# A retention layer and a gated feed-forward on one core: one load, two gate blocks and a few sums change places in a hand-written order

## The chip, the cores and the metric

One core of a Trainium2 chip. The metric is device time in microseconds of one execution. The program is built from a language in which each instruction goes to the queue of one engine (TensorE, VectorE, ScalarE, GpSimd, SyncE) in the order in which the program issues it; semaphores between the engines are set from the data that they share.

## The reference

Two layers, one after the other, on q, k, v of (4 batches, 8 heads, 768 steps, 64):

```python
gamma = 1.0 - 2.0 ** (-5.0 - np.arange(H))
for t in range(S):
    state = gamma * state + np.einsum('bhd,bhe->bhde', k[:, :, t], v[:, :, t])
    y[:, :, t] = scale * np.einsum('bhd,bhde->bhe', q[:, :, t], state)
x = y.transpose(0, 2, 1, 3).reshape(B * S, H * D)          # 3072 x 512
gate = 1.0 / (1.0 + np.exp(-(x @ w_gate)))                 # w_gate 512 x 1536
val = x @ w_val                                            # w_val  512 x 1536
out = (gate * val) @ w_out                                 # w_out 1536 x 512
```

## The kernel before, in words

**Chunks, pairs, tiles.** The 768 steps are cut into six chunks of 128, one for each tile `t` (0 to 5). A tile has the four batches of a chunk, so 512 tokens, in two *pairs* `P = 2t` and `2t + 1` of two batches each; `c` (0, 1) is the batch within a pair. So pairs 2 and 3 are tile 1, pairs 4 and 5 are tile 2.

**The first layer for a pair.** `load` (L96, GpSimd's queue) brings k, q, v of a pair from DRAM. k and q are turned: pairs 0 to 3 by TensorE (`tp`, L200) with a copy out of the accumulator by ScalarE (`te`, L210), later pairs by a transposing DMA from SyncE's queue (`xk`, `xq`). `sc` (L238) computes the scores of one batch into two accumulator banks, `mk` (L243, VectorE) multiplies a bank by the decay mask, `in` (L253) multiplies q by the state so far, `ia` (L258) adds masked scores times v, `yo` (L273, VectorE) writes the result as the tile's `xT`. `kt` scales k by the decay, `sm` (L280) computes the new part of the state into the one bank `z`, `zs` (L290, VectorE) adds it to the state and `zo` (L295, ScalarE) writes it out for the matmuls.

**The second layer for a tile.** Early tiles: `gm`/`vm` (whole blocks of gate and value, 512 tokens) with `sg` and `mu`, or half blocks of 256 tokens: `ag`, `av` (left half of the columns), `bg`, `bv` (right half), each with sigmoid (`as`, `bs`) and product (`am`, `bm`). From tile 2 on, the products of gate, value and output are done in seven block products in place of eight (Strassen and Winograd's scheme): `gp`, `vp`, `dp`, with the sums of blocks that it needs: of weights (`aw`, `ad`, `dw`, `dd`, `wp`; `ad` and `dd` on VectorE, the others on GpSimd, L361 and L456), of x (`xs` on VectorE, `xg` on GpSimd, L371), of the hidden layer (`hs` on VectorE, `hg` on GpSimd, L474). `gc`, `vc`, `dc` (ScalarE) copy a product out of its bank, `ga`, `va`, `da` (VectorE) add the next to it.

**The order** is written out by hand: `ORDER` has one string for each tile, and each token is a step and its number. `tp7` is number 7 = 2P + i: q (i = 1) of pair 3; `mk10` is 4P + 2c + i: pair 2, batch 1, first bank; `sc`, `in`, `ia`, `yo` count 2P + c; `sm`, `zs` count pairs; `ag2` starts with hidden block 2. A `-` or `+` behind a token moves its tile number by one. A step in capitals does its matmuls whole (128 rows by 128 columns of the array), in small letters as two halves of 64 columns (L305 and L309 in `mm`):

```python
for i in range(2):
    half = slice(i * D, (i + 1) * D)
    nc.tensor.matmul(o[half], left[:, half], right, skip_group_check=True, **kw)
```

**Memory.** Every accumulator bank but `z` comes from `bank()`: the string `PLACES["ff"]` says which of seven banks the next request gets, and its first writer waits until the bank's last tenant has been read. `PLACES["st"]` does the same for the masked scores. The loads of k, q and v of pairs 2 to 5 and of the output weights are issued ahead of `ORDER` on GpSimd's queue; the sums that GpSimd does follow in the same queue.

Of the kernel before, what the change touches and what calls it, by code (L numbers as in the profile page):

```python
# [17 lines left out]
def kernel(  # L18
# [38 lines left out]
        "gs": "01234501234503215034203502345102354130524301453201540321453034035412031524",  # L57
        "maskd": "01",
        "ff": (
            "012345601230465102346523105246310542631405314056321602341562034163412045632516523560132601562306"  # L60
            "251062562015020324512065630653102651604250142343624015405400652016203541034046326504510416035253"
            "245132541351025162405034123406520512341234160532120605410531324"
        ),
        "qkT": "010231230123",
        "kt": "0101100101",
        "st": "012345670123456702134675120346752104637563245710",
        "xT": "010101",
        "hT": "010101",
        "scr": "010101101001101010010101010101",
# [12 lines left out]
    def held_in(P, n):  # L82
        held = {"k": kn, "q": qn, "v": vn}[n]
        t, j = divmod(P, 2)
        if (n, t) not in lands:
            lands[n, t] = place(ld, [C, 4 * H, D], BF16, tag=n, name=n + "n")
        for i in range(2):
            held[2 * t + i] = lands[n, t][:, i * 2 * H:(i + 1) * 2 * H, :]
        return held[P]

    def load(P, *what, pairs=1):
        t, j = divmod(P, 2)
        for n in what:
            held_in(P, n)
            x = {"k": k, "q": q, "v": v}[n]
            nc.gpsimd.dma_start(out=lands[n, t][:, j * 2 * H:(j + pairs) * 2 * H, :],  # L96
                                in_=x[2 * j:2 * (j + pairs), :, t * C:(t + 1) * C, :].rearrange("b h s d -> s (b h) d"))
# [85 lines left out]
    qkT, kt, sc, st, y, zz, za, xT = {}, {}, {}, {}, {}, {}, {}, {}  # L183
# [377 lines left out]
    def hold(P):  # L561
        nc.gpsimd.tensor_copy(kept[:, :2], qkT[P][:, :, 1, NP - 1, C - 1])

    def hold_for_sums(t):
        nc.gpsimd.tensor_copy(kept[:, 2:3], hs[t][:, 2, NFF // 2 - 1, :1])
# [53 lines left out]
    for s in range(4):  # L619
        load_out(s)  # L620
    load(4, "k", "q", "v")
    load(5, "k", "q", "v")

    STEPS = {
        "gm": lambda t, n: up(t, n, 0),
# [38 lines left out]
        "lk": lambda t, P: load(P, "k", pairs=2),  # L664
        "lq": lambda t, P: load(P, "q", pairs=2),
        "lv": lambda t, P: load(P, "v", pairs=2),
        "ho": lambda t, P: hold(P),
        "hi": lambda t, n: hold_for_sums(t),
        "xk": lambda t, P: xbar(P, 0),
# [128 lines left out]
```

## Time and profile before

| | |
|---|---|
| median of 3 runs | 215.74 us (215.36 to 215.93) |
| profiled execution | 215.9 us, of which the span from first to last instruction is 214.2 |
| granted TensorE clock | 1.00 |
| instructions | 7187 |
| busy: TensorE, VectorE, ScalarE, GpSimd | 204.6, 189.2, 147.5, 139.5 us |
| moved by DMA | 25.38 MB, mean 118 GB/s |

Rows below have the start from the span's beginning, the duration, the engine (PE = TensorE, PEld = its weight loads, DVE = VectorE, ACT = ScalarE, POOL = GpSimd, SP = SyncE), the line of the kernel, the operation and its tiles as out<-in, the shapes, and the count of instructions merged into the row. What stands in brackets is the idle time of the engine just before, and what ended it. The chain of waits follows the run back from its last instruction, at each step to what released it.

### The profile page before, as it was taken

What the parts mean: (1) busy time and instruction counts of PE and PEld (TensorE: products, weight loads), DVE (VectorE), ACT (ScalarE), POOL (GpSimd) and SP (SyncE); (2) the same over time, 40 slices, a digit from 0 to 9 for tenths busy, and PEclk for the clock granted to TensorE, in tenths of its full rate; (3) what the DMA queues carried; (4) which work ended last, traced back from release to release, by engine and by line L of the source; (5) the groups of instructions that cost most, each with busy time, mean ns of one, the idle gap of its engine ahead of it and who ended that gap; (6) DMA issues with size and microseconds to landing.
All of it is one profiled execution on the core that took longest, in us unless ns stands there. A gap on an engine that the chain in (4) does not pass through costs nothing.

```text
span 214.2 us, 7187 instructions
## 1 busy us (share of the span) xinstructions
PE 204.6 (96%) x2938; PEld 177.3 (83%) x2938; DVE 189.2 (88%) x406; ACT 147.5 (69%) x396; POOL 139.5 (65%) x145
## 2 busy tenths in 40 slices
PE   6778999999999999999999999999999999999994
PEld 6555555778888998899988889998899988888883
DVE  6587979989999999979999899999999999968971
ACT  6384466543994389786869798787768969577731
POOL 8977784679999946699764279875618537024500
PEclk9999999999999999999999999999999999999999
DMA  9999999999995999969995129998121000023305
GB/s 125 143 170 194 195 173 165 183 199 159 159 132 33 98 156 143 204 126 157 170 227 115 49 99 163 159 105 127 49 101 52 3 0 3 0 50 70 75 25 183
DMA packets 103922, 25.38 MB, mean 118 GB/s; under 512 B 93904, under 2 KB 101072, under 8 KB 103888
## 3 DMA queue, kind: packets, MB, share of 16 engines
q0 software_dynamic: 81104, 13.90, 84.6%
q1 hardware_dynamic: 22640, 10.88, 28.6%
q8 instruction: 23, 0.38, 0.7%
q10 hardware_dynamic: 144, 0.13, 0.2%
q14 instruction: 11, 0.09, 0.1%
HBM read 28.31 MB, written 6.29 MB: 162 GB/s over the span
## 4 chain that ended last, share of the span: by engine, by line
PE 76%; DMA 14%; POOL 4%; DVE 3%; issue 1%; ACT 0%; ACTq 0%; DVEq 0%; POOLq 0%
PE ff L305 41%; PE ff L309 29%; DMA qn<-in_q_dram 6%; DMA wg<-in_moe_w_gate_dram 4%; DMA vn<-in_v_dram 4%; PE ff L238 2%; PE ff L258 2%; DVE scr L414 1%; POOL kn L96 1%; PE z L280 1%; DVE gs L435 1%; DVE xT L273 1%; POOL vn L96 1%; POOL qn L96 1%; POOL kn L104 1%
## 5 line engine op out<-in xcount | busy, mean ns | idle before, releaser
L420 POOL TENSOR_TENSOR hT<-gs,scr 128x512 bf16<-128x512 f32 x17 | 22.1, 1302 | 21.4 <-ACT gs L440 9.0
L430 ACT COPY gs<-ff 128x256 f32<-128x256 f32 x72 | 25.6, 377 | 11.1 <-PE ff L305 5.7
L409 ACT COPY scr<-ff 128x256 f32<-128x256 f32 x72 | 25.2, 375 | 6.5 <-PE ff L309 3.6
L414 DVE TENSOR_TENSOR scr<-scr,ff 128x512 f32<-128x512 f32 (+1 forms) x48 | 25.6, 547 | 3.5 <-ACT scr L409 1.3
L435 DVE TENSOR_TENSOR gs<-gs,ff 128x512 f32<-128x512 f32 (+1 forms) x48 | 25.8, 548 | 3.2 <-PE ff L305 2.0
L510 ACT COPY ob<-ff 128x256 f32<-128x256 f32 x48 | 17.7, 375 | 15.2 <-PE ff L305 8.9
L243 DVE TENSOR_TENSOR st<-ff,maskd 128x512 bf16<-128x512 f32 x40 | 25.7, 682 | 0.9 <-PE ff L238 0.9
L440 ACT ACTIVATE gs<-gs 128x512 f32<-128x512 f32 (+1 forms) x48 | 24.7, 530 | 2.3 <-DVE gs L435 2.2
L309 PE MATMUL ff<-xT,wg 128*64 128x256 bf16 (+1 forms) x268 | 24.2, 308 | 0.0
L309 PEld LDWEIGHTS <-wg 128*64 128x64 bf16 x356 | 19.4, 110 | 4.1 <-issue 0.4
L423 POOL TENSOR_TENSOR hT<-gs,scr 128x256 bf16<-128x256 f32 x16 | 11.9, 747 | 15.9 <-ACT gs L440 12.0
L309 PE MATMUL ff<-xT,wv 128*64 128x256 bf16 (+1 forms) x220 | 21.5, 311 | 0.0
L305 PEld LDWEIGHTS <-hT 128*128 128x128 bf16 x198 | 19.2, 98 | 2.7 <-issue 0.2
L305 PE MATMUL ff<-wo,hT 128*128 128x256 bf16 x156 | 21.0, 273 | 0.0
L309 PEld LDWEIGHTS <-wv 128*64 128x64 bf16 x312 | 17.2, 110 | 4.2 <-issue 0.3
L305 PEld LDWEIGHTS <-wv 128*128 128x128 bf16 x184 | 17.7, 98 | 2.4
L305 PEld LDWEIGHTS <-wg 128*128 128x128 bf16 x162 | 15.7, 98 | 3.8 <-issue 1.1
L309 PE MATMUL ff<-xs,ws 128*64 128x256 bf16 x208 | 18.7, 273 | 0.0
L305 PE MATMUL ff<-xT,wv 128*128 128x256 bf16 (+1 forms) x134 | 18.5, 276 | 0.0
L231 ACT ACTIVATE kt<-kn,tabk 128x128 bf16<-128x128 bf16 x48 | 18.3, 405 | 0.1
L309 PEld LDWEIGHTS <-ws 128*64 128x64 bf16 x308 | 17.2, 110 | 0.3
L305 PE MATMUL ff<-xT,wg 128*128 128x256 bf16 x110 | 15.4, 272 | 1.6 <-ACT xT L271 1.6
(118 smaller groups left out, 526.8 us busy)
## 6 DMA issues: line engine op xcount, KB each, us to landing
out_dram<-ob SPq DMA_DIRECT2D x18, 256.0 KB, 3.3
vn<-in_v_dram POOLq DMA_DIRECT2D x6, 256.0 KB, 12.4
wo<-in_moe_w_out_dram POOLq DMA_DIRECT2D x4, 384.0 KB, 14.2
kn<-in_k_dram POOLq DMA_DIRECT2D x3, 512.0 KB, 7.8
qn<-in_q_dram POOLq DMA_DIRECT2D x3, 512.0 KB, 10.0
vn<-in_v_dram POOLq DMA_DIRECT2D x3, 512.0 KB, 11.6
out_dram<-ob SPq DMA_DIRECT2D x11, 128.0 KB, 2.2
kn<-in_k_dram POOLq DMA_DIRECT2D x5, 256.0 KB, 13.4
```

The costliest lines, as they stand in the source:

```text
L231: nc.scalar.activation(to[:, :, h, :], x[:, :, h, :], AX.Copy, scale=tabk[:, 0, h:h + 1])
L243: nc.vector.tensor_tensor(st[P, c, i], sc[P, c][i], (mask0 if P < 2 else maskd)[:, i], op=ALU.mult)
L305: nc.tensor.matmul(o, left, right, skip_group_check=True, **kw)
L309: nc.tensor.matmul(o[half], left[:, half], right, skip_group_check=True, **kw)
L409: nc.scalar.copy(vals[t, g][:, {1: 0, 5: 2, 3: 1}[n]], m[False][:, 256:] if n == 1 else m[True][:, :256])
L414: nc.vector.tensor_tensor(o, o, x, op=ALU.add)
L420: eng.tensor_tensor(h[:, 2 * g], s, vals[t, g][:, 0:2].rearrange("p two n -> p (two n)"), op=ALU.mult)
L423: eng.tensor_tensor(h[:, 2 * g + 1, 256:], s[:, 256:], vals[t, g][:, 2], op=ALU.mult)
L430: nc.scalar.copy(o, pairs[t, g, 0][x][:, :256] if x else pairs[t, g, 0][x][:, 256:])
L435: nc.vector.tensor_tensor(o, o, pairs[t, g, 0][False][:, cols], op=ALU.add)
L440: nc.scalar.activation(o, x, AX.Sigmoid)
L510: nc.scalar.copy(o, fast[t, i][x][:, :256] if x else fast[t, i][x][:, 256:])
```

## The change

Five edits of the order, and one string of places made to match.

1. The load of v for pair 5 is no longer issued with the other loads; a new step `lw` issues it behind `hg6` of tile 0 (a hidden sum on GpSimd).
2. At the end of pair 2: the four masks stand together and in the order 10, 11, 8, 9; `in4` in halves takes the place of `IN4`, ahead of both `ia` steps; the products `mu10` and the block `vm11` stand behind `yo4`.
3. The gate block `ag2` stands ahead of the transposes of pair 3's q (`tp7`), `ag4` ahead of pair 3's scores (`sc6`, `sc7`), and the value block `AV6` ahead of `ia6`, `ia7`.
4. `dc11` and `dc15` of tile 0 stand ahead of `kt46` and `kt44` on ScalarE, `hs7` ahead of `dd17` and `bm4` on VectorE; `xs2` of tile 2 and the weight sum `dd3` stand ahead of sums of tile 1's hidden layer (`hs9`, `hs11`).
5. In tile 2, `sm6` stands behind `gp57` and `gs57` and not ahead of `vp47`.

`PLACES["ff"]` and `PLACES["st"]` are new from the first such step on. Apart from names of banks, the tenants ahead of a request differ only around edits 2 and 3 and around `AV4` to `AV10` of tile 1.

```diff
-    load(5, "k", "q", "v")
+    load(5, "k", "q")
...
+        "lw": lambda t, P: load(P, "v"),
...
-mu6- mu8- mk10- mk8- mk11- wp8 vm10- mu10- wp2 in5 ia5 vm11- IN4 mk9- ia4 yo5 tp6 yo4 aw13 sg11- te6 mu11-
-tp7 te7 dd5 dd15 ag2 ag6 kt24 xk5- as2 sc6 mk12 dd20 sc7 mk15 sm3 ag4 as4 wp5 dd7 ag0 IN7 zs3 VM7- as0 mk13
-mk14 IN6 zo7 sm2- zs2 ia6 yo6 ia7 yo7 AV6 zo4 AV2 AG10
+mu6- mu8- mk10- mk11- mk8- mk9- wp8 vm10- wp2 in5 in4 ia5 ia4 yo5 yo4 vm11- mu10- tp6 aw13 sg11- te6 mu11-
+ag2 tp7 te7 dd5 dd15 ag6 kt24 xk5- as2 ag4 sc6 mk12 dd20 sc7 mk15 sm3 as4 wp5 dd7 ag0 IN7 zs3 VM7- as0 mk13
+mk14 IN6 zo7 sm2- zs2 AV6 ia6 yo6 ia7 yo7 zo4 AV2 AG10
...
-zo6 hg6- BV0
+zo6 hg6- lw5 BV0
...
-bs6 kt46 kt44 dc11- AV4 kt37 am0 BV6 bm0 bm2 wp10 xq5- hs11- dd17 bm4 dc15- hs7- DP13-
+bs6 dc11- dc15- kt46 kt44 AV4 kt37 am0 BV6 bm0 bm2 wp10 xq5- hs11- hs7- dd17 bm4 DP13-
...
-hs8 zo11 gp25+ vc01+ hs9 | hs11- gp21 gp22 xs2 gp01 gp02 ... dp17-- gc05 dd3- gc01
+hs8 dd3 zo11 gp25+ vc01+ xs2+ hs9 | hs11- gp21 gp22 gp01 gp02 ... dp17-- gc05 gc01
...
-vf46 vf56 sm6 vp47 va47 in14 gp57 ga57 gs57 vp57
+vf46 vf56 vp47 va47 in14 gp57 ga57 gs57 sm6 vp57
```

More of the change, by code (lines that the diff above doesn't have):

```diff
@@ L59 @@
         "ff": (
-            "012345601230465102346523105246310542631405314056321602341562034163412045632516523560132601562306"
-            "251062562015020324512065630653102651604250142343624015405400652016203541034046326504510416035253"
-            "245132541351025162405034123406520512341234160532120605410531324"
+            "012345601230465102346523105246310542631405314056321632045631205431542056312643621634012430462136"
+            "240362462304323125402364613641032640635243052151625304534533642306231450315356126435403506314241"
+            "254012450140324062534315021536423402150215063412023634503410125"
         ),
@@ L65 @@
         "kt": "0101100101",
-        "st": "012345670123456702134675120346752104637563245710",
+        "st": "012345670123456701234675210346751204637563145720",
         "xT": "010101",
```

54 rows, old and new, of the table ORDER are left out of this document.

## The prediction

> **What bounds the kernel now.** I read the engines of the page first, then the chain of waits, then the timelines of TensorE, VectorE, ScalarE and GpSimd around the changed steps, and last the DMA issues.
>
> ```profile
> PE 204.6 (96%) x2938; PEld 177.3 (83%) x2938; DVE 189.2 (88%) x406; ACT 147.5 (69%) x396; POOL 139.5 (65%) x145
> ```
>
> TensorE is busy almost throughout; a gain has to show as a wait that it no longer has, or as matmuls that it issues more cheaply. The chain of waits says where the last wait for data is:
>
> ```profile
> 27.54 13.44 DMA qn<-in_q_dram
> ```
>
> That is pair 3's q: it lands at 27.54 + 13.44 = 40.98 us. From there on the chain is nearly all TensorE, with short pieces of VectorE. The stretch that is changed, in TensorE's timeline (start, us, line, xcount):
>
> ```profile
> 37.08 1.03 PE L309 MATMUL ff<-xT,wv 128*64 128x512 bf16 x8
> 37.94 0.39 PE L309 MATMUL ff<-qkT,zbd 128*64 128x128 bf16 x8
> 38.16 0.52 PE L258 MATMUL ff<-st,vn 128*64 128x128 bf16 x8
> 38.49 1.05 PE L309 MATMUL ff<-xT,wv 128*64 128x512 bf16 x8
> 39.48 0.40 PE L305 MATMUL ff<-qkT,zbd 128*128 128x128 bf16 x4
> 39.81 0.41 PE L258 MATMUL ff<-st,vn 128*64 128x128 bf16 x8
> 40.05 0.61 PE L200 MATMUL ff<-ident,kn 128*64 128x128 bf16 x16
> 41.02 0.64 PE L200 MATMUL ff<-ident,qn 128*64 128x128 bf16 x16 [0.36 <-DMA qn<-in_q_dram]
> 41.49 1.91 PE L309 MATMUL ff<-xT,wg 128*64 128x256 bf16 x32
> 43.34 0.62 PE L238 MATMUL ff<-qkT 64*128 64x128 bf16 x16
> 43.89 0.44 PE L280 MATMUL z<-vn,kt 128*64 128x64 bf16 x16
> 44.16 1.92 PE L309 MATMUL ff<-xT,wg 128*64 128x256 bf16 x32
> 46.01 0.40 PE L305 MATMUL ff<-qkT,zbd 128*128 128x128 bf16 x4
> ...
> 47.43 0.44 PE L280 MATMUL z<-vn,kt 128*64 128x64 bf16 x16
> 47.70 0.62 PE L258 MATMUL ff<-st,vn 128*64 128x128 bf16 x16
> 48.25 1.92 PE L305 MATMUL ff<-xT,wv 128*128 128x256 bf16 x16
> ```
>
> In step names these are vm10, in5, ia5, vm11, IN4, ia4, tp6, tp7, ag2+ag6, sc6+sc7, sm3, ag4+ag0, IN7, (VM7, IN6), sm2, ia6+ia7, AV6+AV2. Ends are modelled and overlap the next start, so I count from start to start. A wait for data shows at tp7 only, and all that is gained before 40.98 is worth nothing unless tp7 stops being the next thing that TensorE must do.
>
> **Pair 2's end, up to the first transposes (tp6).** IN4 becomes in4: four full matmuls become eight halves, like in5. in5 takes 38.16 - 37.94 = 0.22 us. IN4 takes 39.81 - 39.48 = 0.33, and vm11 ahead of it takes 39.48 - 38.49 = 0.99 where vm10, of the same form, takes 0.86: 0.13 goes into the change of form. So in4 saves 0.33 + 0.13 - 0.22 = 0.24. ia5 takes 0.33 where ia4 takes 0.24, because its second matmul waits for mask mk11; with mk11 second among the masks that 0.09 goes too. Against it stands a new wait: ia4 now follows ia5 at once and needs the fourth mask, mk9.
>
> ```profile
> 36.36 1.89 DVE L243 TENSOR_TENSOR st<-ff,maskd 128x512 bf16<-128x512 f32 x3
> ```
>
> Three masks in 1.89 us, one of 0.68: a step of 0.605. Four in a row from 36.36 end at 36.36 + 3 x 0.605 + 0.68 = 38.86. TensorE would begin ia4 at 37.94 + 0.22 + 0.22 + 0.24 = 38.62 and finish it at 38.86 + about 0.25 = 39.1. vm11 (0.86) ends at 39.97, so tp6 starts at 39.97, not 40.05: only 0.08 is gained here. What is queued on VectorE behind these masks is yo5, yo4 and, moved behind them, mu10 and mu11; yo4 ends near 39.3 + 0.7 = 40.0 (a step as long as a mask's). Nothing asks for mu10 or mu11 before sc6 takes their banks at 43.6.
>
> **Gate blocks ahead of pair 3's q and scores.** tp6 takes what tp7 takes, 41.49 - 41.02 = 0.47, and ends at 40.44. ag2 (needs yo5 and yo4, done at 40.0) now fills the time until q has landed: a half block is about 0.87 (two take 1.85, of which 0.10 goes to the change of form into the scores). It ends at 41.31, after 40.98, so tp7 doesn't wait: 41.31 to 41.78. ag6 ends at 42.65, ag4, also moved up, at 43.52, and sc6 starts at 43.62. The copies out of the transposes run under those blocks:
>
> ```profile
> 40.71 2.01 ACT L210 COPY qkT<-ff 128x1024 bf16<-128x1024 bf16 x2 [2.34 <-PE ff L200]
> ```
>
> One takes 1.0; the second can start at about 41.95 and ends at 43.0, ahead of 43.62. If this cover were gone (tp7 0.6 later), the scores would wait. sc6, sc7 and sm3 take 44.16 - 43.34 = 0.82, so ag0 starts at 44.44, against 44.16 + 0.87 = 45.03 before: a lead of 0.59. IN7 follows after 46.01 - 45.03 = 0.98 at 45.42, and sm2 after another 1.42 at 46.84.
>
> **AV6 ahead of ia6 and ia7.** sm2 has one accumulator bank, which zs3 must have read.
>
> ```profile
> 43.77 0.69 DVE L243 TENSOR_TENSOR st<-ff,maskd 128x512 bf16<-128x512 f32 x1 [0.68 <-PE ff L238]
> ```
> ```profile
> 45.38 1.12 DVE L290 SCALAR_TENSOR_TENSOR za<-za,tabz,z 128x128 f32<-128x128 f32 x4
> 46.41 1.28 DVE L243 TENSOR_TENSOR st<-ff,maskd 128x512 bf16<-128x512 f32 x2
> 47.91 1.12 DVE L290 SCALAR_TENSOR_TENSOR za<-za,tabz,z 128x128 f32<-128x128 f32 x4 [0.22 <-PE z L280]
> ```
>
> VectorE waited for the scores at 43.77; they come 43.62 - 43.34 = 0.28 later, so zs3 ends at 46.50 + 0.28 = 46.78, just in time for sm2, and the masks for ia7 end at 47.69 + 0.28 = 47.97. In the old order ia7 would stand at about 47.3 and wait 0.6; AV6 fills that. Its price is two more changes of form: ia6+ia7 to AV6 costs about 0.10 (48.25 - 47.70 = 0.55 for two times 0.22), and a return about as much, so 0.22 together. sm2 46.84 to 47.11, AV6 from 47.23 to 48.10, ia6 and ia7 from 48.20 to 48.64, AV2 at 48.76, against 48.25 + 0.87 = 49.12. **The lead that is left is 0.36 us.** The Trainium skill ("TensorEngine Tiling (Array Packing)", Key Properties) says that changing the tiling mode drains the engine; by it alone, IN4 to in4 saves two changes, AV6 adds two, and that pair would come to nothing. The rows agree that a change costs; the gain of this part comes from tp7's wait.
>
> VectorE has no lead here (zs2 begins at 47.9 in both) and needs none: yo7 is done near 50.3, and the first block on the right half of the columns follows AV2, AG10 and a product, at about 51.2.
>
> **Pair 5's v load.** On GpSimd's queue:
>
> ```profile
> 46.41 1.14 POOL L96 DMA_DIRECT2D vn<-in_v_dram  x1 [0.59 <-DMA wo<-in_moe_w_out_dram]
> ```
> ```profile
> 60.77 1.34 POOL L474 TENSOR_TENSOR hT<-hT 128x512 bf16<-128x512 bf16 x1
> ```
>
> Without it the queue goes on at 46.41 - 0.59 = 45.82, not at 47.55: every sum up to hg6 comes 1.73 earlier, hg6 ends at 62.11 - 1.73 = 60.38, and the load is issued there; what is behind it is up to 0.6 earlier. No gain of TensorE's follows, since it doesn't wait for these sums. The load's first reader is sm5:
>
> ```profile
> 69.58 0.44 PE L280 MATMUL z<-vn,kt 128*64 128x64 bf16 x16
> ```
>
> With the lead this is 69.22, so the load may take 8.8 us from issue to landing.
>
> ```profile
> vn<-in_v_dram POOLq DMA_DIRECT2D x6, 256.0 KB, 12.4
> ...
> kn<-in_k_dram POOLq DMA_DIRECT2D x3, 512.0 KB, 7.8
> ```
> ```profile
> vn<-in_v_dram POOLq DMA_DIRECT2D x1, 256.0 KB, 17.5
> ```
>
> The last row is this load itself, in its old place, at the end of a full queue. The bounds are 7.8 (twice the bytes, median of three later loads) and 17.5. At 60.38 only q of pair 5 is ahead of it, so I take 7.8 or less: landing by 68.2, cost nothing, about 1 us to spare.
>
> **The rest.** dc11, dc15 ahead of two kt, hs7 ahead of dd17, and xs2 and dd3 ahead of hidden sums reorder the same work on ScalarE and VectorE; they let TensorE's readers come 0.36 earlier without finding them late.
>
> ```profile
> 78.19 0.42 DVE L371 TENSOR_TENSOR xs<-xT,xs 128x512 bf16<-128x512 bf16 x1
> 78.52 0.29 DVE L361 TENSOR_TENSOR ws<-wg,ws 128x256 bf16<-128x256 bf16 x1
> ```
>
> I cost them at nothing; bounds are +-0.7, the two rows' sum, should a reader of one or of what they displace stand waiting. sm6 moved behind gp57:
>
> ```profile
> 109.02 0.61 DVE scr L414
> 109.62 0.04 issue
> 109.67 0.41 PE ff L309 x4
> ```
> ```profile
> 109.11 0.41 PE L309 MATMUL ff<-xs,wg 128*64 128x256 bf16 x4
> ```
>
> gp57 to vp57 takes 0.56 where the four matmuls need 0.22: 0.34 of waiting for VectorE (va56). sm6 can fill 0.25 of it, but gp57 in turn has to wait for the addition that ends at 109.02, so it can't move up, and vp57 starts when va56 ends, as before. Taken as nothing, bounds 0 and -0.34. Does VectorE keep the lead until there?
>
> ```profile
> 97.63 0.42 DVE L516 TENSOR_TENSOR ob<-ob,ff 128x256 f32<-128x256 f32 x1 [0.23 <-PE ff L309]
> ```
>
> Its last wait before 109.6 is one for TensorE, so it comes earlier with it. The sum is -0.36, rounded to -0.35. The profiled execution took 215.9 us (214.2 span); with the change 215.55. The median of the runs is 215.74, so **215.4 us**.
>
> **The rivals.**
>
> *VectorE runs ahead as well (faster).* A sum on VectorE takes 1.23 us beside GpSimd's sums where a like one took 0.29 above:
>
> ```profile
> 51.85 1.23 DVE L361 TENSOR_TENSOR ws<-wv,ws 128x256 bf16<-128x256 bf16 x1
> ```
>
> GpSimd's sums now lie partly beside masks and its load beside dd17, so VectorE may lose up to 1.23 - 0.29 = 0.94 less for each sum so freed. Were the wait at 109.67 to vanish, it is -0.35 - 0.34 = -0.7; with one more like it in a later tile, -1.05: 214.7 to 215.05. For it: sums of this kind are many. Against: VectorE waits for TensorE at 97.63, so what it wins before then is lost in that wait.
>
> *The load lands after sm5 (slower).* It decides from 8.8 us on. At 12.4 the landing is at 72.8, TensorE waits 3.6 and the kernel ends 3.2 later, at 218.9; at 17.5, at 77.9 and 8.3 later. A landing only 1 to 2 us too late gives 216.4 to 217.4. For it: the median row of v. Against: those loads stood in a full queue. The Trainium skill ("SBUF — State Buffer", section "SBUF: two separate sides") warns that VectorE in a two-port mode locks GpSimd out of writing a load's descriptors; "Who interferes with whom" excepts tensor_tensor, which is what runs on VectorE there. No run here shows such a lock on this load yet.
>
> *The lead is given back (no change).* The new waits for mk9 and zs3 are tight to 0.1 us, and VectorE has no lead at 47.9; if TensorE finds one of its results late by 0.35 before 58, the time is 215.7.
>
> **How the numbers follow.** A measurement of this kernel can tell about 0.3% (0.65 us) from no change. The forecast, -0.35 with its own range of 215.1 to 215.7, has 0.37; the lead given back 0.05: together within 0.3%, 0.42. VectorE ahead too, 0.35: faster by over 0.3%; I give it much, since every reordered sum points that way. The late load 0.23: slower. The range of 8 in 10 runs from 214.5 (all of the second case and 0.2 for the scatter of the runs) to 216.8 (a load late by a little over 1 us); a load that is later is left out.
>
> **What would show it.** In TensorE's timeline tp7 without a wait, near 41.3; ia4 with one of about 0.25; AV2 near 48.8; sm5 near 69.2 with no wait for v; the step to vp57 near 109.3 still waiting. v of pair 5 issued near 60.4 and landed by 68.2. The prediction is wrong if tp7 still waits, if AV2 stands at 49.1 or later, or if a wait for v stands ahead of sm5.

## The result, and the profile after

| | kernel before | changed kernel |
|---|---|---|
| median | 215.69 us (215.36 to 215.93, 4 runs) | 220.27 us (217.13 to 224.45, 4 runs) |
| ratio, 95% interval | | 1.0072 (1.0049 to 1.0094) |
| profiled execution | 215.9 us, span 214.2 | 223.13 us, span 221.4 |

The change makes the kernel slower by 0.7%, about 1.5 us, where 0.35 us less was forecast. The executions of both kernels fall into a lower and an upper group (223 to 229 us in 5 of 35 later executions of the kernel before, 220 to 224 us in 8 of 12 of the changed one); the ratio compares the lower groups, and the profiled execution (223.13 us) is from the upper one. So the rows below don't show how the 1.5 us are made up; that is read from the edited kernels further on.

TensorE's timeline of the changed kernel, up to the place where it goes wrong:

```profile
38.53 0.61 PE L309 MATMUL ff<-qkT,zbd 128*64 128x128 bf16 x16
38.98 0.90 PE L258 MATMUL ff<-st,vn 128*64 128x128 bf16 x16
39.69 1.05 PE L309 MATMUL ff<-xT,wv 128*64 128x512 bf16 x8
40.55 0.64 PE L200 MATMUL ff<-ident,kn 128*64 128x128 bf16 x16
41.00 1.06 PE L309 MATMUL ff<-xT,wg 128*64 128x256 bf16 x16
41.87 0.64 PE L200 MATMUL ff<-ident,qn 128*64 128x128 bf16 x16
...
45.99 0.40 PE L305 MATMUL ff<-qkT,zbd 128*128 128x128 bf16 x4
...
47.09 0.39 PE L305 MATMUL ff<-qkT,zbd 128*128 128x128 bf16 x4
51.09 0.57 PE L280 MATMUL z<-vn,kt 128*64 128x64 bf16 x16 [3.62 <-DVE za L290]
51.60 1.89 PE L305 MATMUL ff<-xT,wv 128*128 128x256 bf16 x8
```

tp7 (41.87) no longer waits, and IN7 is at 45.99 although this execution was 0.59 us behind from 18.6 us on. Then sm2 waits 3.62 us for zs3. VectorE's timeline says why zs3 is late:

```profile
45.54 0.68 DVE L243 TENSOR_TENSOR st<-ff,maskd 128x512 bf16<-128x512 f32 x1
46.14 3.87 DVE L361 TENSOR_TENSOR ws<-wg,ws 128x256 bf16<-128x256 bf16 x1
49.93 1.11 DVE L290 SCALAR_TENSOR_TENSOR za<-za,tabz,z 128x128 f32<-128x128 f32 x4
```

The middle row is dd7, a weight sum that takes 0.28 us elsewhere: it takes 3.87. Beside it, on GpSimd:

```profile
44.69 1.14 POOL L96 DMA_DIRECT2D qn<-in_q_dram  x1 [0.82 <-DMA wo<-in_moe_w_out_dram]
45.85 0.68 POOL L361 TENSOR_TENSOR ws<-wv 128x256 bf16<-128x256 bf16 x1
46.49 1.16 POOL L456 TENSOR_TENSOR wt<-wo 128x512 bf16<-128x512 bf16 x1
47.60 1.15 POOL L456 TENSOR_TENSOR scr<-wo 128x512 f32<-128x512 bf16 x1
48.71 1.14 POOL L456 TENSOR_TENSOR wt<-wo 128x512 bf16<-128x512 bf16 x1
50.04 1.15 POOL L456 TENSOR_TENSOR wt<-wo 128x512 bf16<-128x512 bf16 x1 [0.19 <-DMA wo<-in_moe_w_out_dram]
```

The first row is the load of pair 5's q, the others are sums. With the load of v gone from the queue, the sums start at 45.85, in place of 47.56 before, and run without a pause to 49.85. dd7 stands from 46.14 and ends at 50.01: it got its turn when GpSimd paused for 0.19 us. In the kernel before, VectorE's zs3 starts at 45.38, so dd7 and dd20 are through before GpSimd's first sum:

```profile
45.18 0.28 DVE L361 TENSOR_TENSOR ws<-wg,ws 128x256 bf16<-128x256 bf16 x1
```
```profile
47.56 0.68 POOL L361 TENSOR_TENSOR ws<-wv 128x256 bf16<-128x256 bf16 x1
```

The wait costs twice. The busy time by stretch (us; then busy time and count of PE, PEld, DVE, ACT, POOL; granted clock, DMA) has TensorE's clock at 0.54 of full speed just behind it:

```profile
51.00:54.00 3.00, 2.90 (x36) 2.06 (x38) 2.27 (x7) 1.31 (x3) 1.94 (x3) 0.54 2.48 156
```

A second place follows at pair 4's scores:

```profile
69.62 0.61 PE L305 MATMUL ff<-wo,hs 128*128 128x256 bf16 x4 [0.31 <-DVE hs L474]
...
71.37 0.38 PE L238 MATMUL ff<-qkT 64*128 64x128 bf16 x7 [0.98 <-DVE hT L349]
71.97 0.40 PE L238 MATMUL ff<-qkT 64*128 64x128 bf16 x8 [0.22 <-DVE hT L349]
```
```profile
65.91 3.66 DVE L474 TENSOR_TENSOR hs<-hT,hs 128x512 bf16<-128x512 bf16 x2
69.49 1.23 DVE L361 TENSOR_TENSOR ws<-ws,wg 128x256 bf16<-128x256 bf16 x1
```

hs11 and hs7 take 3.66 us (0.84 on a quiet GpSimd), dd17 1.23, and bm4 and am4, for which the second bank of sc8 and then sc9 wait, stand behind them. The same three sums lost time in the kernel before, too, but less; hs11, dd17 and hs7 there:

```profile
60.52 0.57 DVE L474 TENSOR_TENSOR hs<-hT,hs 128x512 bf16<-128x512 bf16 x1
61.01 1.24 DVE L361 TENSOR_TENSOR ws<-ws,wg 128x256 bf16<-128x256 bf16 x1
...
62.77 0.78 DVE L474 TENSOR_TENSOR hs<-hT,hs 128x512 bf16<-128x512 bf16 x1
```

This is how far each TensorE step starts from its start in the kernel before, worked out from the timelines (minus is earlier):

```
step    before  changed  load_back load_alone dd7_early sums_clear load_first
in5      37.94   +0.59     +0.02     -0.10     +0.18     +0.32      -0.03
IN7      46.01   -0.02     -0.60     -0.12     -0.33     -0.30      -0.65
sm2      47.43   +3.66     -0.60     -0.12     -0.09     -0.30      -0.65
AV2      49.13   +5.28     -0.38     -0.12     +0.13     -0.09      -0.43
DP13     63.54   +5.39     -0.12     -0.12     +0.14     -0.08      -0.42
sc9      64.53   +7.45     +0.08     -0.12     +1.52     -0.08      -0.42
dp01     72.93   +7.45     +0.09     -0.12     +1.53     -0.08      -0.42
gp15     79.95   +7.46     +0.09     +0.74     +1.53     +0.59      -0.42
gp17     85.79   +7.40     +0.04     +0.93     +1.48     +1.05      +0.23
gp01 t3 111.55   +7.29     -0.08     +0.90     +1.36     +1.03      +0.19
last DP 210.18   +7.20     -0.17     +0.89     +1.27     +0.94      +0.1
```

The 7.2 us of this execution are 0.6 from the start, 3.7 at sm2, 1.5 from there to DP13 at the lowered clock (5.39 - 3.66, less the 0.22 that the prediction estimates for AV6's two changes of form), 2.1 from DP13 to sc9, less TensorE's lead of 0.4 and about 0.25 won back later.

### The profile page after: what moved, and what is told of

Same layout as the page of the kernel before. It is cut to its first block, busy times and chain, and to the rows that moved or that the text cites. A ratio compares the mean times of both kernels' runs of the same rounds, so it can differ in the third digit from the quotient of the medians.

```text
span 221.4 us, 7194 instructions
## 1 busy us (share of the span) xinstructions
PE 207.3 (94%) x2941; PEld 179.3 (81%) x2942; DVE 192.1 (87%) x406; ACT 147.4 (67%) x396; POOL 139.0 (63%) x145
## 4 chain that ended last, share of the span: by engine, by line
PE 83%; DVE 13%; issue 1%; ACT 1%; ACTq 0%; DVEq 0%
PE ff L305 38%; PE ff L309 34%; PE ff L238 3%; DVE ws L361 3%; PE ff L258 3%; PE ff L537 2%; PE ff L200 2%; DVE st L243 1%; DVE hs L474 1%; DVE hT L349 1%; PE z L280 1%; DVE hT L332 1%; DVE scr L414 1%; ACT xT L271 1%; DVE qkT L210 1%
## 5 line engine op out<-in xcount | busy, mean ns | idle before, releaser
L305 PE MATMUL ff<-xT,wv 128*128 128x256 bf16 (+1 forms) x133 | 19.6, 285 | 0.1
L295 ACT CAST zbd<-za 64x512 bf16<-64x512 f32 x20 | 12.3, 616 | 8.2 <-DVE za L290 6.0
```

The lines of the kernel that those rows point to most:

```text
L295: nc.scalar.copy(zbd[P % 2][half, :, :, half], za[P % 2][half])
L305: nc.tensor.matmul(o, left, right, skip_group_check=True, **kw)
```

## The experiments

Theory A: VectorE's sums whose two inputs both lie in SBUF can't run beside GpSimd's sums, and may lose their turn several times; the moved load lets GpSimd's sums run into dd20, dd7 and what follows. Rivals: the new order costs by itself (B), or v lands late (C). C falls at once: v of pair 5, issued at 66.82, landed in 4.8 us.

```profile
vn<-in_v_dram POOLq DMA_DIRECT2D x1, 256.0 KB, 4.8
```

**The changed kernel once more.** No edit.

> The changed kernel once more, unaltered, for the scatter of its times and a second profile. Theory A (the weight sum dd7 on VectorE, with both inputs in SBUF, can't get in between GpSimd's sums, which now run back to back from 45.8 us; zs3 and so sm2 on TensorE wait behind it): dd7 takes between 0.9 and 4 us instead of 0.28, TensorE waits between IN6 and sm2 for as much less 0.2, and the time scatters from 216.5 to 224.5 with the number of GpSimd's sums that dd7 waits out. Theory B (the new order on TensorE and VectorE costs by itself): the same time in each run, 217 us, with waits at ia4 or ia6. Theory C (pair 5's v lands late): a wait at sm5.

221.58 us median of 12 runs (216.92 to 223.78), ratio 1.006 (1.0015 to 1.0104). In its profile (220.41 us) dd7 takes 0.64, dd20 0.73, the wait ahead of sm2 is 0.8 and that at the scores 2 us. The same two places, with another share each: as A says, and a fixed cost (B) doesn't do that.

**The load back in its old place, all else changed.**

```diff
-    load(5, "k", "q")
+    load(5, "k", "q", "v")
...
-zo6 hg6- lw5 BV0
+zo6 hg6- BV0
```

> The changed kernel with pair 5's v load back among the early loads; all the other edits stay. Theory A: dd7 is done in 0.3 us before GpSimd's sums begin at 47.5 us, sm2 doesn't wait, and the lead of 0.35 us is left: 215.3 to 215.5 us with as little scatter as the kernel before. Theory B: still 217 us or more. Theory C: 215.4 us too, but with dd7 short in the changed kernel's own profile.

215.68 us median of 12, ratio 0.9987 (0.9957 to 1.0017). dd7 in VectorE's timeline:

```profile
45.45 0.28 DVE L361 TENSOR_TENSOR ws<-wg,ws 128x256 bf16<-128x256 bf16 x1
45.65 1.12 DVE L290 SCALAR_TENSOR_TENSOR za<-za,tabz,z 128x128 f32<-128x128 f32 x4
```

The load's move is the loss; without it the rest of the change can't be told from the kernel before. TensorE's lead at AV2 is 0.38 us, as forecast, but it is gone by sc9: BG2 waits 0.25 us for am2, behind hs4 (1.41 us) and ad11 (1.24), and sc9 0.2 for am4.

**The load's move alone, on the kernel before.**

```diff
-    load(5, "k", "q", "v")
+    load(5, "k", "q")
...
+        "lw": lambda t, P: load(P, "v"),
...
-zo6 hg6- BV0
+zo6 hg6- lw5 BV0
```

> The kernel before with nothing changed but pair 5's v load, which is issued behind hg6. Theory A: dd7 stands at 45.2 to 45.5 us here, ahead of GpSimd's sums, which begin at 45.8, so it mostly escapes: 215.4 to 216.0 us; where it comes 0.4 us later it is caught, and a run is 1 to 8 us slower. Theory B: 215.7 us. Theory C: 217 us or more with a wait for v at sm5.

218.22 us median of 12, ratio 1.0094 (1.0062 to 1.0127). dd7 escapes (0.28 us at 45.06), as A says, but the time does not stay: the expected 215.4 to 216.0 was wrong. There is a third place. VectorE and GpSimd:

```profile
74.68 1.48 DVE L371 TENSOR_TENSOR xs<-xT 128x512 bf16<-128x512 bf16 x1
```
```profile
74.25 0.68 POOL L361 TENSOR_TENSOR ws<-wv,ws 128x256 bf16<-128x256 bf16 x1
74.88 1.72 POOL L96 DMA_DIRECT2D vn<-in_v_dram  x1
```

xs0, 0.43 us elsewhere, meets GpSimd's sum aw7, which in this queue stands later against VectorE; gp05, gp01 and gp03 then wait, 0.84 us in all (-0.12 to +0.72). aw7 alone doesn't account for the row: it ends at 74.93, and xs0 at 76.16, so some 0.8 us of its delay fall beside the load's issue. This execution (216.78 us) is the fastest of the twelve; what the others lost on top of it isn't shown.

**dd7 ahead of the masks.**

```diff
-sc6 mk12 dd20 sc7 mk15 sm3 as4 wp5 dd7 ag0
+sc6 dd7 mk12 dd20 sc7 mk15 sm3 as4 wp5 ag0
```

> The changed kernel, load moved and all, with dd7 put ahead of mask mk12 on VectorE, where that engine waits 1.2 us for the scores; it runs then at 43.4 us, before GpSimd has any sums. Theory A: dd7 takes 0.28 us, zs3 ends at 46.5, sm2 doesn't wait: 215.2 to 215.5 us without scatter. Theory B and C: 217 us and more, as the changed kernel.

217.35 us median of 12, ratio 1.0065 (1.0032 to 1.0098): the expected time was missed, the expected step not. dd7 takes 0.28 us at 42.98; its neighbour dd20 now takes 0.73, so sm2 waits 0.24 and not 0.8 to 3.6; but dd17 waits at the second place, and sc8 and sc9 with it (the row is sc8's second bank; sc9 starts 1.52 later than before):

```profile
62.44 2.36 DVE L361 TENSOR_TENSOR ws<-ws,wg 128x256 bf16<-128x256 bf16 x1
```
```profile
65.45 0.38 PE L238 MATMUL ff<-qkT 64*128 64x128 bf16 x7 [0.80 <-DVE hT L349]
```

The ratio is that of the changed kernel (1.0072 and 1.006): with sm2's wait nearly gone, the loss is no smaller. So these times aren't owed to sm2 alone.

**The load behind GpSimd's first or second sum.** `lw5` behind `aw12+`, or behind `wp0+`, in place of behind `hg6-`.

> The changed kernel with pair 5's v load not behind hg6 but behind the first of GpSimd's sums, aw12. Theory A (VectorE's sums with two inputs in SBUF wait for GpSimd's sums): only aw12 (0.65 us) and then the load, which is no sum, stand beside dd20 and dd7, so dd7 is done by 46.9 us and sm2 waits 0.3 us or less; hs7 and dd17 wait as in the kernel before, about 1.3 us each: 215.3 to 215.9 us. Theory A' (a load's issue on GpSimd blocks them as well): dd7 waits to the load's end, 47.7 us, sm2 waits 1 us: 216.2 to 216.8 us.

> The changed kernel with the load behind the second of GpSimd's sums, wp0. Theory A: dd7 waits out at most aw12 and wp0, to 47.7 us, and sm2 waits 0 to 1.1 us, more than with the load behind aw12: 215.4 to 216.7 us. Theory A': to the load's end at 48.8 us in the worst case, 217.5 us.

Behind aw12: 216.41 us median of 10, ratio 0.9994 (0.9961 to 1.0028); dd7 takes 0.55, and sm2 starts 0.07 later than before where IN6 was 0.69 earlier. That is a wait of 0.76, between the 0.3 of A and the 1 us of A'. Part of it neither form foresaw: dd20 took 0.77, beside nothing but the issue of pair 5's q load:

```profile
44.57 0.77 DVE L361 TENSOR_TENSOR ws<-wg 128x256 bf16<-128x256 bf16 x1
```
```profile
44.41 1.14 POOL L96 DMA_DIRECT2D qn<-in_q_dram  x1 [0.95 <-DMA wo<-in_moe_w_out_dram]
45.57 0.68 POOL L361 TENSOR_TENSOR ws<-wv 128x256 bf16<-128x256 bf16 x1
```

Behind wp0: 219.38 us median of 4, ratio 1.0064 (1.004 to 1.0088), above what A allowed. The order of the two is as expected; the sizes are not told apart well, since the second profile was already 3.3 us behind at 38 us, dd20 and dd7 (0.65 and 0.71) met other sums there, and kt24, a product of two SBUF inputs, took 3.38 us (1.22 elsewhere), for which sm3 waited 1.32.

**Three weight sums out of GpSimd's way, load behind hg6.**

```diff
-sc6 mk12 dd20 sc7 mk15 sm3 as4 wp5 dd7 ag0
+sc6 dd20 dd7 mk12 sc7 mk15 sm3 as4 wp5 ag0
...
-hs7- dd17 bm4
+hs7- bm4
...
-hs8 dd3 zo11
+hs8 dd3 dd17 zo11
```

> The changed kernel, load behind hg6, with three weight sums of VectorE taken out of GpSimd's way: dd20 and dd7 ahead of mask mk12 (VectorE idle, GpSimd without sums) and dd17 beside dd3 at about 78 us. Theory A: dd20 and dd7 take 0.28 us each, sm2 doesn't wait, am4 comes earlier by the 1.2 to 2.4 us of dd17, and the wait at sc9 (1.4 us with dd7 alone moved) falls under 0.5: 215.2 to 216.0 us. If the cost were in anything else of the change, it stays at 217 us.

216.25 us median of 10, ratio 1.0025 (0.9998 to 1.0053), a little above the 216.0 expected; the slowest of the ten is 218.16, where the changed kernel reached 223.78. Neither sm2 nor sc9 waits (the table: -0.30 and -0.08), so the first two places are closed by moving three sums of VectorE, with the load where the change put it. The third, xs0 with 1.48 us, is still there, and the last tenths of the loss are its: VectorE's next additions for gate blocks start 1.05 us later than before (81.11 against 80.06), and TensorE loses 0.67 from dp01 to gp15 and 0.46 more up to gp17.

**Does a load's issue hold VectorE up, too?** The kernel just shown, with the sum aw7 behind tile 3's v load.

```diff
-lq6- aw7- kt59
+lq6- lv6- aw7- kt59
...
-vc05 lv6- gp15
+vc05 gp15
```

> The run with three weight sums moved clear and the load behind hg6, with GpSimd's sum aw7 moved behind tile 3's v load, so that nothing but loads stands beside xs0 of tile 2, which took 1.48 us there instead of 0.43 and cost TensorE 0.6 us. If only sums hold VectorE up: xs0 takes 0.43 us and the time is 215.2 to 215.9 us. If a load's issue does too: xs0 takes 0.7 to 1.5 us and the time is 216 to 216.8 us.

```profile
74.38 0.43 DVE L371 TENSOR_TENSOR xs<-xT 128x512 bf16<-128x512 bf16 x1
```
```profile
73.73 1.68 POOL L96 DMA_DIRECT2D vn<-in_v_dram  x1
75.42 0.69 POOL L361 TENSOR_TENSOR ws<-wv,ws 128x256 bf16<-128x256 bf16 x1
```

xs0 takes 0.43 us in the middle of the load's issue: the issue doesn't hold it up here. But xs0 began 0.65 us into the load, and dd20 of the run behind aw12 began 0.15 into one and was held. In all the profiles together, 249 two-input SBUF sums of VectorE began beside a load that was followed by another load, and none was held; beside a load right ahead of GpSimd's first sum, four that began 0.15 to 0.54 us into it were each held until about 0.65. So the question stays open for loads next to GpSimd's sums.

The time is 216.21 us (6 runs), ratio 1.0036 (1.0013 to 1.0059), above the 215.9 expected: TensorE keeps its lead of 0.42 to gp15 and has lost 0.65 by gp17. The wait is at VP23, a block product shortly ahead of gp17. It waits for ScalarE's copy vc25, which stands behind sigmoids that waited for VectorE's addition ga27, and this stands behind xs3, one more two-input sum:

```profile
85.10 0.38 PE L305 MATMUL ff<-xT,ws 128*128 128x256 bf16 x2 [0.18 <-ACT scr L409]
```
```profile
83.29 0.94 ACT L440 ACTIVATE gs<-gs 128x256 f32<-128x256 f32 x2 [0.46 <-DVE gs L435]
```
```profile
81.50 0.77 DVE L371 TENSOR_TENSOR xs<-xT,xs 128x512 bf16<-128x512 bf16 x1
```

xs3 took 0.77 in the kernel before, too, where a like sum takes 0.42 alone. So closing three places uncovers a fourth, worth less.

**GpSimd busy, but reading nothing.** aw12, wp0, wp1 and wp4 are left out; zeros are written to their tiles instead (the edit for the last three is shown; aw12's, with two writes, is alike).

```diff
-        nc.gpsimd.tensor_tensor(o, x, z, op=op)
+        if (g, i) in ((0, 0), (0, 1), (1, 0)):
+            for _ in range(3):
+                nc.gpsimd.memset(o, 0.0)
+            return
+        nc.gpsimd.tensor_tensor(o, x, z, op=op)
```

> The changed kernel in which GpSimd's first four sums (aw12, wp0, wp1, wp4) are left out and GpSimd writes zeros to the same tiles instead, two or three times each, so that it is busy with instructions that write SBUF but read nothing. Theory A in the form that only GpSimd's reads hold VectorE's second input up: dd20 and dd7 take 0.28 us each although GpSimd is busy beside them, and sm2 doesn't wait (under 0.1 us). Theory A in the form that any instruction of GpSimd does: dd7 takes 0.5 to 4 us as in the changed kernel. The time itself isn't compared, since GpSimd's work differs.

```profile
45.00 0.28 DVE L365 TENSOR_TENSOR ws<-wg,ws 128x256 bf16<-128x256 bf16 x1
```
```profile
44.87 0.70 POOL L363 MEMSET ws<- 128x256 bf16 x2
45.51 1.69 POOL L462 MEMSET wt<- 128x512 bf16 x3
```

dd7 takes 0.28 us wholly beside GpSimd's writing, and sm2 doesn't wait. That is the row for a rule of the Trainium skill ("SBUF — State Buffer", section "Who interferes with whom"): a VectorE instruction with two inputs in SBUF contends with a GpSimd instruction that reads SBUF, and not with one that only writes it. The run agrees. dd20 ran ahead of the zeros, so this rests on one instruction.

**Four sums clear, and the load back; and a fifth.** The first moves dd20, dd7, dd17 and ad11, the second dd18 as well (shown are the new places of the first four).

```diff
-sc6 mk12 dd20 sc7 mk15 sm3 as4 wp5 dd7 ag0
+sc6 dd20 dd7 mk12 sc7 mk15 sm3 as4 wp5 ag0
...
-vc01+ xs2+ hs9
+vc01+ xs2+ dd17 ad11 hs9
```

> The load back among the early loads, and four weight sums of VectorE out of GpSimd's way: dd20 and dd7 ahead of mk12, dd17 and ad11 behind xs2 at about 78 us, where GpSimd has nothing for 3 us. Theory A: the lead of 0.37 us at AV2 isn't lost at BG2 (0.25 in the run with the load back) nor at sc9 (0.2), but the two sums come ahead of tile 1's hidden sums: 214.9 to 215.4 us. If the lead is lost elsewhere anyway: 215.5 to 215.8 us.

215.6 us median of 10, ratio 0.9996 (0.9972 to 1.002), above the 215.4 expected. TensorE holds -0.43 us up to gp15 and still has -0.27 at the end; the span is 213.9 against 214.2. Within the interval it can't be told from the kernel before, nor from the run with the load back.

> The kernel with the load back and four weight sums clear of GpSimd's, with a fifth, dd18, moved behind ga16. Theory A: that kernel's TensorE kept a lead of 0.43 us up to 84 us and lost 0.28 at gp17, which waits for ga16 behind VectorE's queue; with dd18 0.28 later the lead stays near 0.4 to the end: 215.1 to 215.4 us, faster than the kernel before by 0.1 to 0.2%. If the lead is lost at the next result instead: 215.4 to 215.7 us.

216.12 us median of 12, ratio 1.0002 (0.9989 to 1.0016): no gain. The rows of the run before it say why: 0.27 of the lead was lost at VP23, as above, ahead of gp17 and not at it, and dd18 stands behind ga27 in VectorE's queue, so its place has no bearing on that wait. Its profiled execution (222.96 us) is the clearest row of all, with the load in its old place:

```profile
54.97 9.80 DVE L474 TENSOR_TENSOR hs<-hs,hT 128x512 bf16<-128x512 bf16 x2
```
```profile
54.95 1.15 POOL L456 TENSOR_TENSOR scr<-wo 128x512 f32<-128x512 bf16 x1
...
63.50 0.66 POOL L361 TENSOR_TENSOR wg<-wg 128x256 bf16<-128x256 bf16 x1
```
```profile
65.77 0.61 PE L305 MATMUL ff<-wt,hs 128*128 128x256 bf16 x2 [5.66 <-DVE hT L349]
```

The first of two hidden sums (0.84 us together elsewhere) began as GpSimd began the first of ten sums without a pause, and ended 0.3 us after the tenth. TensorE waited 5.66 us. So the load's old place doesn't keep the kernel safe from such a wait.

## Why the prediction was wrong

- *TensorE's steps*: right. tp7 didn't wait; IN7 came 0.60 earlier (forecast 0.59), AV2 0.38 (0.36), both with the load back. ia4's new wait was 0.26 (0.25).
- *"No gain of TensorE's follows, since it doesn't wait for these sums"*: this is the step that failed. GpSimd's sums were moved 1.7 us earlier and only their readers were asked, not what they run beside. I named no cover for that edit. The cover was the load itself: its issue kept GpSimd's sums away from VectorE while dd20, dd7 and zs3 ran. Taken at nothing, it measured 3.6 us at sm2 in one profile and 0.8 in another, and about 2 us at pair 4's scores in both.
- *"zs3 ends at 46.78, just in time for sm2"*: the margin of under 0.1 us was seen, but its operands were not: dd20 and dd7 ahead of zs3 in the queue are of the very kind whose 1.23 us was shown as a row.
- *That row* was used with the wrong sign: as what VectorE might be freed of (rival "VectorE runs ahead"), and as a price of 0.94 us for one sum. It is no upper bound: a sum can lose several turns, 3.87 and over 9 us.
- *The section of the Trainium skill* that the late-load rival drew on ("SBUF — State Buffer", "Who interferes with whom") was read for its exception alone. The same section has the rule that mattered, for sums and not for loads.
- *The load*: it landed in 4.8 us, under the 7.8 taken; that rival's mechanism is not what happened, though its sign was.
- *"The rest", at nothing with +-0.7*: sm6 right (vp47 0.27 earlier in the run with the load back, vp57 only 0.08). The bound was too narrow for hs7 and dd17: about 2 us at the second place.
- *Range*: 216.8 left out what the second and third place add. The scatter came with it: in the two profiles of the changed kernel GpSimd's first sum began at 45.85 and at 45.08, and dd7 took 3.87 and 0.64.

## What to carry to other kernels

Whoever moves something in one engine's queue also moves everything behind it against the other engines: list what will stand beside it, not only who reads it. A load in GpSimd's queue may be the gap that lets VectorE's two-input SBUF sums through. Such sums belong where GpSimd waits, writes only or issues one load after another, and not ahead of an instruction that TensorE waits for; right ahead of GpSimd's next sum, a load's issue was no safe cover (dd20's 0.77 us).

## What the runs showed of the hardware that was not expected

A two-input SBUF sum on VectorE doesn't just wait for the one GpSimd sum in progress: it can miss the turn at each boundary as long as GpSimd's sums follow one another, three times in the changed kernel (3.87 us) and nine times in the last run (over 9 us), and slip in after one sum at other times (1.2 us). What decides a turn stays open. Such losses are not new with the change: counting the two-input SBUF sums and products of VectorE that took over 1.2 times the shortest of their shape, the kernel before has 15 that lost 8.6 us together, the changed kernel 12 with 11.7 us in its first profile and 10 with 7.5 in its second. What the change moved is which of them TensorE has to wait for.

And a wait of 3.6 us on TensorE is followed by a stretch at a granted clock of 0.54, which cost another 1.5 us; the Trainium skill ("TensorE: Matmul & The Clock Gate", Part 1) says that the gate sets the clock by how busy the array has been, and that row agrees. The wait need not be that long: in the second profile the clock is at 0.57 from 68 to 72 us, behind waits of 0.32, 0.98 and 0.22 us at pair 4's scores.
